# Attention and gated MLP on one core: v split in the layout of its product, gate in one step, 8 pairs instead of 12 transposed by TensorE

## The chip, the core and the metric

The kernel runs on one core of a Trainium2 chip. The core has TensorE (PE in the profile; PEld is its weight load), VectorE (DVE), ScalarE (ACT), GpSimd (POOL) and SyncE (SP), which here only issues DMAs. Every engine works through its own list of instructions in order. The metric is the device time of one execution in microseconds (us), the median of several runs.

## The reference, cut to what matters

```python
def _attn_ref(q, k, v, w1, b1, w2):            # B, H, S, D = 8, 8, 576, 64
    scores = 1/np.sqrt(D) * np.matmul(q, k.transpose(0, 1, 3, 2))
    rel = (pos[:, None] - pos[None, :])
    x = np.log1p(np.abs(rel)) / np.log1p(np.maximum(pos[:, None], 1.0))
    bias = np.maximum(x[..., None] @ w1 + b1, 0.0) @ w2       # [S, S, H]
    scores = scores + bias.transpose(2, 0, 1)[None]
    attn = exp(scores - max); attn = attn / (attn.sum(-1) + 1e-9)
    return np.matmul(attn, v)

def _moe_ref(x, w_val, conv_w, w_out):         # x: [8, 576, 512], 5 taps
    gate_pre = sum(conv_w[k] * xp[:, k:k + S, :] for k in range(5))
    gate = 1.0 / (1.0 + np.exp(-gate_pre))
    return gate * (x @ w_val) @ w_out
```

The attention output of the 8 heads, laid side by side, is the x of the second function.

## The kernel before

**Pairs.** The attention is done in 32 pairs of heads (8 batches, 4 pairs each). A pair n has four blocks c of 128 query rows; the 64 rows that are left of two successive pairs share a fifth block. For each block TensorE makes the logits (L698, L714 for the fifth), VectorE adds the bias and takes the row minimum (`logits`, L744), ScalarE takes the exponential with its row sum (`expo`, L756). So the logits (L744) come 18 to every two pairs, 288 in all, and they are used below as a clock: "the 54th logits" ends the sixth pair.

**T pairs and D pairs.** The exponentials must be turned before they are multiplied with v. `TRANS` says how, for two pairs at a time. In a T pair ("T" in `TRANS`; 12 of 32 before: pairs 0 to 7, 16, 17, 24, 25) they are normalised (`norm`, L801), turned by TensorE in float32, nine 128x128 squares a block (`tp`, L846), copied out of PSUM (`tev`, L206), and multiplied with v in float32 (`piece`, L915; `rem_mm`, L983). In a D pair (20 before) ScalarE casts them to float16 (`top`, L206), GpSimd or VectorE takes the rest that the cast lost (`rest`, `rest8`, L229), SP issues a DMA transpose of high and low part together, 18 squares (`swap`, L880, L883), TensorE multiplies float16 products (L915, L983), and the row sums are spread by small matmuls (`rb`, L960, L992) and multiplied in afterwards (`mu`, L970).

**v of a D pair** is loaded with head dimension on the partitions (L630), its maximum is taken for each partition (L633), it is scaled and split into two float16 parts (L646, L649), and both are turned by a DMA transpose of 10 squares (`vtr`, L660).

**MLP.** When the four pairs of a batch are done, the five taps of the convolution run (`taps`, L1104, and L1064, L1069), then the gate: a tanh (`sig`, L1116) and a step that makes a scaled sigmoid of it (`half`, L1121 on ScalarE, L1123 on the others, for each of 4 slices of 128 channels). TensorE multiplies x with w_val in three float16 products (L1170), VectorE multiplies by the gate (`gf`, L1180), the product is split (L206, L229) and multiplied with w_out (L1225).

**Order.** Nothing is scheduled at run time: `ORDER` is a compressed table that lists the tasks in the order in which they are recorded, and the engine of each one that can run on more than one. Buffers come from rings of the sizes in `BUFS`. The first part of the program makes the bias rows and stores them to DRAM (L328 to L393); they are read back from there (L415).

Of the kernel before, what the change touches and what calls it, by code (L numbers as in the profile page):

```python
# [12 lines left out]
F16 = mybir.dt.float16  # L13
# [30 lines left out]
TRANS = tuple(x == "T" for x in "TTTTDDDDTDDDTDDD")  # L44
BUFS = dict(w=13, d=6, pt=2, sp=2, ps=4, qk=2, rel=3, be=9, xp=2, xh=1, gh=1, gx=1)
ORDER = (
    'c-nPW0cav;n|60cGue!Bl8nhDnPex)BpJ<QGf5_!Nix}5u;35&a1RSE*ux$!_=7zxSg?l$d$@-M3+~~91s5#X!v+7t9`<m-9v1A6|6vac?qPo{Sg>Hhg8i{z!5;U1WA^WVaQEtb-'
    '}^q#^S<AV^L^ipI7tyMk5`o4^+r>J(G06_e5>7&y1jm_;cM2}p#Pmf#A3DCb5V!0)oaINiFBcuFC_;<Jk=kKGqy6+uxH~{-sup9aHlJcuVHj78BZ{-Trppf1$Tk-'
    '1*$CPNu_(4tUp*P*Z5GsG8~K)TfNe>G+K6tQ*iNuD209A_FJz<YIx8u;}q$!R>vJ8mk$*cn$Q$t@uVeD>h)6tX2a$jmieyTL5_Z@&{6+2S2!Ix=?R&-'
    '$jJS{aOB1binLOmL9L0^8zm(cx6n+k#Z~*!MuPPvQ{#NG(DnxXye3d83u0EPbsCk8P&guo6syf)X*RuBz140<!nSBE>2$g6j!fRgb+Vp#!kNl-al(&Py<{{%`r>J#Q09u1Sb65A1)gHWwKwd;jJKQa'  # L50
    'NOF+%Rb%Bq!kTS;=kE>rlEOtSsnJ+t(F8DSkPTVGG9JYgdYd2G@bm~zjs?O_*c{GlBAIcCb*q%k=O~h*8L4(wsyS?pmeMQ~?UqE$S#~eKdJki{cBeS*_Te77;>onfTk56YCi+U1<e<zrs~SI@%8cBZ'
    '^l<!fF4%Z0oX8hLShLkGL}O*a<>pI~Y-dm*NSg6{=Xu)m`uqW}uVNE}Oukx^{6E+&R3K=Tm9VqhD>yzKuv{qAAGn4;^KMVE5(>X7MzHEbd%f{qX;>cN<C-'
    'L2*2dntMwBX54erAPS$W=i7z>6hR*SVj6r<%zxZN%J1Mx&MA}gJgH5Q+vzDOj~>0l;PqnWIwSC?%zyOPc23n521mroT0mg`6Cj-mW%X%KyXBueG7#Tj=vd7;_zHQKfg+@x-'
    '($3$ESt2>#qJ1QI1m?vM$Wb2JoJRKeQy}pt&;Hp%c{lREB8rMdT+%3&;luXqlX$?MZf7R4<Fpn4W`H8?>HxtYT!x-KoNUA`EqIj(L14q<y^<ue7=ZmsJa*>LOqHB#0XeQBK8^S8-'
    'jM2|($9vuWmkqu%7zV>pmP_(N3MO}2lroZH-RNo@PFEykiP_|Qp+z;by*SIcJ>J}_ZHL~;_XTp$=_(0#Pjq?R6k2;8AHycosf-713@wN~&LPRwRKC#9=A4Sx&wrTCKB-'
# [55 lines left out]
PACE = (3.35, 1.88, 2, 1)  # L111
PARTS = ((0, 256), (256, 320))
TOP = 2.0**12
GDIV = 2.0**20
LEAST = float(np.array([0x38000000], np.uint32).view(np.float32)[0])


# [1207 lines left out]
```

## Time and profile before

| what | value |
|---|---|
| median of 3 runs | 693.33 us (692.54 to 694.25) |
| the profiled execution: its own time, its span | 698.68 us, 696.2 us |
| TensorE matmul busy | 659.1 us (95% of the span) |
| VectorE, ScalarE, GpSimd busy | 623.7 (90%), 593.1 (85%), 457.3 us (66%) |
| DMA queue of SP (q1) | 80.5% of 16 engines |
| mean granted TensorE clock | 0.995 |

The span is the time from the first to the last instruction of the profiled execution. Busy times are the union of an engine's instructions; two instructions that overlap on one engine count once, so the mean durations of groups add up to more than the busy time. The DMA share is the sum of the packets' times over 16 engines, so it can pass 1 where packets overlap.

### The profile page before, as it was taken

To read this page: it belongs to the slowest core of one execution; us is meant where nothing else is said; L and a number is where in the kernel's file an instruction comes from. 1 tells how busy PE (TensorE), PEld (TensorE's weight loads), DVE (VectorE), ACT (ScalarE), POOL (GpSimd) and SP (SyncE) were. 2 spreads that over 40 slices of the span, in tenths; PEclk is the share of its full clock that TensorE was granted. 3 is DMA by queue.
4 is the path that set the end of the run, shared out by engine and by line. 5 is a ranking of instruction groups with operands and counts; after the bars stand their busy time and mean duration, and the time that the engine had idled before them with its cause. 6 is when DMAs were issued, how large, how long until landed. Compare 5 with 4: busy or idle time off the path is not lost. (4 is left out here: it accounts for less than half of the span.)

```text
span 696.2 us, 17319 instructions
## 1 busy us (share of the span) xinstructions
PE 659.1 (95%) x6144; PEld 418.3 (60%) x6144; DVE 623.7 (90%) x1631; ACT 593.1 (85%) x1332; POOL 457.3 (66%) x637
## 2 busy tenths in 40 slices
PE   6998899999999999899999999988999999999897
PEld 1223576666665666566667766556676666566563
DVE  7999799999999989979988898989898999999862
ACT  6999688888999979978879988879978988999761
POOL 0113656568787778767877787767858888976431
PEclk9999999999999999999999999999999999999999
DMA  3999826322269999999896599999973999999812
GB/s 112 327 320 322 293 104 231 107 93 65 73 121 168 210 214 202 221 189 191 165 203 203 104 184 190 199 220 206 185 187 104 181 217 215 214 188 183 178 63 74
DMA packets 263302, 125.73 MB, mean 181 GB/s; under 512 B 239792, under 2 KB 240048, under 8 KB 263216
## 3 DMA queue, kind: packets, MB, share of 16 engines
q1 hardware_dynamic: 263072, 124.34, 80.5%
q8 instruction: 48, 0.79, 0.5%
q14 instruction: 38, 0.31, 0.2%
q10 hardware_dynamic: 144, 0.29, 0.2%
HBM read 44.64 MB, written 20.33 MB: 93 GB/s over the span
## 5 line engine op out<-in xcount | busy, mean ns | idle before, releaser
L756 ACT ACTIVATE t_d<-t_d,nm 128x576 f32<-128x576 f32 x288 | 222.0, 773 | 33.3 <-DVE nm L744 30.0
L229 POOL TENSOR_TENSOR t_d<-t_d 128x512 f16<-128x512 f32 (+1 forms) x211 | 202.6, 977 | 64.9 <-ACT t_d L206 41.8
L744 DVE CUSTOM_DVE_ANT_0 t_d<-t_sp,bias 128x576 f32<-128x576 f32 x256 | 185.8, 749 | 15.4 <-PE t_sp L698 10.3
L698 PE MATMUL t_sp<-t_qk 64*128 64x288 f32 x1024 | 172.4, 430 | 3.5 <-DMA t_qk<-qkd 1.7
L915 PE MATMUL t_ps<-t_pt,t_w 128*64 128x256 f16 (+1 forms) x1600 | 130.2, 309 | 8.8 <-DMA t_w<-t_w 4.3
L698 PEld LDWEIGHTS t_sp<-t_qk 64*128 64x128 f32 x1024 | 97.8, 186 | 52.2 <-DVE nm L744 15.8
L801 POOL TENSOR_SCALAR t_d<-t_d,rinv 128x576 f32<-128x576 f32 x94 | 75.0, 809 | 45.9 <-DVE rinv L784 35.2
L206 ACT CAST t_d<-t_d 128x576 f16<-128x576 f32 x145 | 94.2, 667 | 8.7 <-DMA t_pt<-t_d 3.0
L1170 PEld LDWEIGHTS <-wv 128*128 128x128 f16 x768 | 72.5, 98 | 32.8 <-issue 12.9
L1170 PE MATMUL t_ps<-xh,wv 128*128 128x320 f16 (+1 forms) x512 | 74.3, 286 | 2.3 <-DVE t_w L213 1.2
L915 PEld LDWEIGHTS <-t_w 128*64 128x64 f16 x1120 | 58.3, 111 | 21.0 <-issue 15.6
L846 PE MATMUL t_ps<-ident,t_d 128*128 128x128 f32 x486 | 67.0, 280 | 3.8 <-POOL t_d L801 2.3
L1104 DVE SCALAR_TENSOR_TENSOR t_ps<-t_xp,convw,t_ps 128x288 f32<-128x288 f32 x126 | 65.3, 518 | 2.7 <-ACT t_ps L1095 0.7
L846 PEld LDWEIGHTS t_ps<-ident,t_d 128*128 128x128 f32 x486 | 52.7, 141 | 24.5 <-POOL t_d L801 8.8
L1225 PE MATMUL t_ps<-wo,gh 128*128 128x512 f16 x256 | 61.5, 380 | 1.1 <-ACT gh L206 0.7
L206 ACT COPY t_pt<-t_ps 128x512 f32<-128x512 f32 (+1 forms) x121 | 53.4, 485 | 4.1 <-PE t_ps L846 3.5
L756 ACT ACTIVATION_READ_ACCUMULATOR t_d<-t_d,nm 128x1 f32 x288 | 55.2, 192 | 0.0
L347 PE MATMUL t_ps<-rel,w 128*32 128x288 f32 (+17 forms) x352 | 46.1, 495 | 4.0 <-DVE t_be L368 2.1
L915 PEld LDWEIGHTS t_ps<-t_pt,t_w 128*64 128x64 f32 x480 | 33.7, 137 | 24.1 <-issue 4.8
L328 DVE TENSOR_SCALAR rel<-gt,sct,nb 128x576 f32<-128x576 f32 (+17 forms) x106 | 47.0, 512 | 0.1
L229 DVE TENSOR_TENSOR t_d<-t_d 128x512 f16<-128x512 f32 (+1 forms) x59 | 41.9, 719 | 3.0 <-ACT t_d L206 2.6
L1225 PEld LDWEIGHTS <-gh 128*128 128x128 f16 x256 | 23.1, 98 | 32.6 <-issue 6.9
(140 smaller groups left out, 1076.8 us busy)
## 6 DMA issues: line engine op xcount, KB each, us to landing
t_qk<-qkd SPq DMA_DIRECT2D x32, 576.0 KB, 4.6
bias_d<-t_be SPq DMA_DIRECT2D x36, 295.5 KB, 4.7
bias<-bias_d SPq DMA_DIRECT2D x16, 576.0 KB, 6.2
out<-t_w SPq DMA_DIRECT2D x32, 256.0 KB, 3.6
t_w<-vd SPq DMA_DIRECT2D x20, 320.0 KB, 3.9
t_w<-vn SPq DMA_DIRECT2D x12, 320.0 KB, 4.7
t_d<-wvd SPq DMA_DIRECT2D x4, 512.0 KB, 3.7
t_d<-wod SPq DMA_DIRECT2D x4, 512.0 KB, 3.6
```

The costliest lines, as they stand in the source:

```text
L206: A.copy(out=out, in_=in_)
L229: (V if e == "V" else G).tensor_tensor(out=out, in0=in0, in1=in1, op=ALU.subtract)
L328: (G if e == "G" else V).tensor_scalar(out=rel[g].t[:, 0:w], in0=src, scalar1=sct[:, mm : mm + 1], scalar2=nb1, op0=ALU.mult, op1=ALU.max,)
L698: T.matmul(ts[a][:, j, 0:hw], lhsT=qk.t[r, c * P : (c + 1) * P], rhs=qk.t[r, x : x + hw], start=True, stop=True,)
L744: V.tensor_tensor_reduce(out=part(c, a).rearrange("p (j f) -> p j f", j=2), in0=sp.t[:, :, 0 : S // 2], in1=bias.rearrange("p (j f) -> p j ...
L756: A.activation(out=part(c, a), in_=part(c, a), func=AF.Exp, bias=nms[c][:, a : a + 1], scale=-1.0, accum_out=sums[c][:, a, 0:1],)
L801: (G if e == "G" else V).tensor_scalar(out=t, in0=t, scalar1=rinvs[c][:, a : a + 1], scalar2=1.0, op0=ALU.mult, op1=ALU.mult,)
L846: T.transpose(t[:, k * P : (k + 1) * P], es[c].t[:, (k0 + k) * P : (k0 + k + 1) * P], ident)
L915: T.matmul(po.t[r, 0:256], lhsT=vt.t[:, v, r], rhs=pt[:, x, :, :] if tr else pt[:, :, x, :], start=(t == 0 and m == 0), stop=(t == 4 and m ...
L1104: V.scalar_tensor_tensor(out=o, in0=x, scalar=wt, in1=t, op0=ALU.mult, op1=ALU.add)
L1170: T.matmul(pm.t[:, 0:w], lhsT=weights["wv"][wi][:, k, d * P : (d + 1) * P], rhs=xb.t[xi][:, k, 0:w], start=(q == 0 and k == 0), stop=(q == ...
L1225: T.matmul(pm.t, lhsT=gb.t[gi][:, k, o : o + P] if o < 256 else gx.t[gi][:, k, :], rhs=weights["wo"][wi][:, k, :], start=(q == 0 and k == ...
```

## The change

- `TRANS` has T for 4 entries instead of 6: pairs 6, 7, 16 and 17 become D pairs (24 D, 8 T).
- v of a D pair is loaded in the layout in which the product needs it (positions on the partitions). Its maximum is still taken for each partition, but one scale holds for the whole pair: TensorE transposes the column of maxima, spread over 128 columns (`vp_mm`, L642), and VectorE takes the maximum of each row (`vp_max`, L646). The two float16 parts are written straight into the tile of the product (`vhi`, `vlo`, L660, L663); `vtr` is gone.
- The gate is (tanh + 1) times the product in one VectorE instruction that reads PSUM (`gf`, L1186); `half` is gone. Its factor for each channel goes into w_val once, at the start: TensorE spreads it over the partitions (`w_cols`, L555), VectorE multiplies it in (`w_even`, L559).
- The scales of the weights and of a batch are turned with transposes in place of matmuls with the identity (L530, L579).
- `norm` of a T pair may run on ScalarE (18 of 72 do).
- Fewer small buffers (`sm` 8 for 16, `nm` and `rinv` 12 for 24, `rinvs` 8 for 10), one more in ring d; `TOP` and `GDIV` are smaller powers of two; `ORDER` is a new table for the new list of tasks.

```diff
-TRANS = tuple(x == "T" for x in "TTTTDDDDTDDDTDDD")
-BUFS = dict(w=13, d=6, pt=2, sp=2, ps=4, qk=2, rel=3, be=9, xp=2, xh=1, gh=1, gx=1)
+TRANS = tuple(x == "T" for x in "TTTDDDDDDDDDTDDD")
+BUFS = dict(w=13, d=7, pt=2, sp=2, ps=4, qk=2, rel=3, be=9, xp=2, xh=1, gh=1, gx=1)
...
-TOP = 2.0**12
-GDIV = 2.0**20
+TOP = 2.0**4
+GDIV = 2.0**12
...
+    def w_cols(e):
+        t = bank(cs)
+        for k in range(NK):
+            T.transpose(t[:, k * P : (k + 1) * P], gsc[:, k : k + 1].to_broadcast([P, P]), ident)
+
     def w_even(e, x, k):
         w = weights["wv"][x][:, k, :]
-        scalars(e, w, w, wrow[2][:, 0, k : k + 1], 1.0)
+        V.scalar_tensor_tensor(
+            out=w, in0=w, scalar=wrow[2][:, 0, k : k + 1], in1=cs.t, op0=ALU.mult, op1=ALU.mult
+        )
...
-            T.matmul(bank(tb)[:, 0:P], lhsT=bsc[:, b, 0:1].to_broadcast([P, P]), rhs=ident, start=True, stop=True)
+            T.transpose(bank(tb)[:, 0:P], bsc[:, b, 0:1].to_broadcast([P, P]), ident)
...
+            def vp_mm(e):
+                T.transpose(bank(tb)[:, 0:P], vcol[:, b, p : p + 1].to_broadcast([P, P]), ident)
+
+            def vp_max(e):
+                t = sc["t"] = smp.tile([P, 4], F32, name="vsc", tag="vsc", bufs=10)
+                V.tensor_reduce(out=t[:, 0:1], in_=tb.t[:, 0:P], op=ALU.max, axis=AX.X)
...
             def vhi(e):
-                A.activation(out=vhl.t[:, 0, :], in_=raw.t, func=AF.Copy, scale=sc["t"][:, 2:3])
+                new(vt, [P, 10, P], F16)
+                A.activation(out=vt.t[:, 0:5, :], in_=raw.t, func=AF.Copy, scale=sc["t"][:, 2:3])
...
-            def vtr(e):
-                new(vt, [P, 10, P], F16)
-                SP.dma_start_transpose(vt.t, vhl.t.rearrange("p a f -> p (a f)"))
-
...
-                A.activation(out=g, in_=g, func=AF.Identity, scale=c, bias=c)
...
-                    V.tensor_tensor(out=gf_.t[:, 0:w], in0=pm.t[:, 0:w], in1=gates[d].t[:, t0 : t0 + w], op=ALU.mult)
+                    V.scalar_tensor_tensor(
+                        out=gf_.t[:, 0:w],
+                        in0=gates[d].t[:, t0 : t0 + w],
+                        scalar=1.0,
+                        in1=pm.t[:, 0:w],
+                        op0=ALU.add,
+                        op1=ALU.mult,
+                    )
```

Three places show how the instructions move. The first is TensorE from the 60th logits on, in the kernel before (t_sp are logits, t_ps<-ident,t_d are squares of exponentials being turned, t_ps<-t_pt,t_w are products with v, t_ps<-t_d,t_w those of the fifth block):

```order
L698 MATMUL t_sp<-t_qk 128x288 x4
L846 MATMUL t_ps<-ident,t_d 128x128 x11
L915 MATMUL t_ps<-t_pt,t_w 64x256 x2
L714 MATMUL t_sp<-t_qk 64x288 x8
L983 MATMUL t_ps<-t_d,t_w 64x64 x10
L915 MATMUL t_ps<-t_pt,t_w 64x256 x18
L698 MATMUL t_sp<-t_qk 128x288 x4
L846 MATMUL t_ps<-ident,t_d 128x128 x8
L983 MATMUL t_ps<-t_d,t_w 64x64 x10
L698 MATMUL t_sp<-t_qk 128x288 x4
L846 MATMUL t_ps<-ident,t_d 128x128 x14
```

The same place in the changed kernel, where L859 is the L846 of before, L928 its L915, L996 its L983, and L642 the new transpose of the column of maxima:

```order
L708 MATMUL t_sp<-t_qk 128x288 x4
L928 MATMUL t_ps<-t_pt,t_w 64x256 x10
L724 MATMUL t_sp<-t_qk 64x288 x8
L859 MATMUL t_ps<-ident,t_d 128x128 x13
L642 MATMUL t_ps<-ident,vcol 128x128
L859 MATMUL t_ps<-ident,t_d 128x128 x5
L708 MATMUL t_sp<-t_qk 128x288 x4
L996 MATMUL t_ps<-t_d,t_w 64x64 x10
L928 MATMUL t_ps<-t_pt,t_w 64x256 x10
L708 MATMUL t_sp<-t_qk 128x288 x4
L996 MATMUL t_ps<-t_d,t_w 64x64 x10
```

The squares of pairs 6 and 7 are gone from here on, and what stands between two sets of logits is shorter.

The second place is SP where the first D pairs begin, before (t_w<-vd loads v, t_pt<-t_d and t_d<-t_d turn exponentials, t_w<-t_w turns v):

```order
L630 DMA t_w<-vd 128x640 x2
L880 DMA_TRANSPOSE t_pt<-t_d 128x18x128 x3
L660 DMA_TRANSPOSE t_w<-t_w 128x10x128
L880 DMA_TRANSPOSE t_pt<-t_d 128x18x128 x2
L608 DMA t_qk<-qkd 128x1152
L1243 DMA out<-t_w 128x512
```

And in the changed kernel:

```order
L636 DMA t_w<-vd 128x640
L893 DMA_TRANSPOSE t_pt<-t_d 128x18x128
L468 DMA t_d<-wod 128x1024
L893 DMA_TRANSPOSE t_pt<-t_d 128x18x128
L636 DMA t_w<-vd 128x640 x2
L615 DMA t_qk<-qkd 128x1152
```

The transposes of v no longer stand between those of the exponentials, and the first of these is issued while weights still load.

The third is VectorE in a D stretch before, from the maximum of one pair's v to the reciprocal of its scale (L633, L637, L643; L744 are logits, L1104 taps):

```order
L633 TENSOR_REDUCE vcol<-t_w 128x1
L1104 SCALAR_TENSOR_TENSOR t_ps<-t_xp,convw,t_ps 128x288 x2
L937 MEMSET t_xp 128x4x4
L1008 TENSOR_TENSOR t_xp<-t_xp,t_ps 128x64
L1104 SCALAR_TENSOR_TENSOR t_ps<-t_xp,convw,t_ps 128x288
L1104 SCALAR_TENSOR_TENSOR t_w<-t_xp,convw,t_ps 128x288
L637 TENSOR_SCALAR vsc<-vcol 128x1
L744 ISA t_d,nm<-t_sp,bias_1_90 128x576
L744 ISA nm 128x1
L643 RECIPROCAL vsc<-vsc 128x1
```

In the changed kernel the same chain has the new maximum over the turned column (L646) in it, before the scale and its reciprocal (L650, L656); between L639 and L646 TensorE must have run L642:

```order
L639 TENSOR_REDUCE vcol<-t_w 128x1
L754 ISA t_d,nm<-t_sp,bias_1_86 128x576
L754 ISA nm 128x1
L754 ISA t_d,nm<-t_sp,bias_1_86 128x576
L754 ISA nm 128x1
L216 SCALAR_TENSOR_TENSOR xl<-t_xp,bsc,xh 128x320 x2
L1021 TENSOR_TENSOR t_xp<-t_xp,t_ps 128x64
L228 TENSOR_TENSOR t_d<-t_d 128x512
L663 SCALAR_TENSOR_TENSOR t_w<-t_w,vsc 128x640
L646 TENSOR_REDUCE vsc<-t_ps 128x1
L650 TENSOR_SCALAR vsc<-vsc 128x1
L656 RECIPROCAL vsc<-vsc 128x1
```

The chain has one more link on VectorE, and two sets of logits and other work now stand between its first and its second maximum.

## Rows read from the trace of the kernel before

**Rows 1.** The page, parts 1 and 2: busy time; DMA share in 40 slices.
```profile
PE 659.1 (95%) x6144; PEld 418.3 (60%) x6144; DVE 623.7 (90%) x1631; ACT 593.1 (85%) x1332; POOL 457.3 (66%) x637
...
DMA  3999826322269999999896599999973999999812
```

**Rows 2.** Busy time by stretch: length; PE, PEld, DVE, ACT, POOL; clock, DMA share, GB/s.
```profile
0.00:154.50 154.50, 138.93 (x1098) 74.85 (x1099) 143.19 (x385) 131.43 (x310) 62.85 (x107) 0.99 0.65 215
154.50:499.30 344.80, 332.82 (x3258) 222.98 (x3257) 314.99 (x829) 306.70 (x685) 264.38 (x349) 1.00 0.90 175
499.30:696.20 196.90, 187.30 (x1793) 120.51 (x1791) 165.50 (x421) 155.01 (x338) 130.09 (x182) 1.00 0.79 164
```

**Rows 3.** Chain that ended last, a stretch of it: start, us, what.
```profile
585.13 1.17 PE t_sp L698 x8
586.30 5.00 PE t_ps L1170 x36
591.30 1.13 PE t_sp L714 x16
```

**Rows 4.** Groups by shape on TensorE: count, busy us, mean ns; idle before.
```profile
L915 PE MATMUL t_ps<-t_pt,t_w 128*64 128x256 f16 x1120 | 71.5, 276 | 6.4 <-DMA t_w<-t_w 4.3 <-DVE t_w L213 0.8 <-ACT t_w L1237 0.5
L846 PE MATMUL t_ps<-ident,t_d 128*128 128x128 f32 x486 | 67.0, 280 | 3.8 <-POOL t_d L801 2.3 <-ACT t_xp L206 0.8 <-ACT t_pt L206 0.2
L915 PE MATMUL t_ps<-t_pt,t_w 128*64 128x256 f32 x480 | 58.8, 387 | 2.4 <-DMA t_w<-vn 2.3
L960 PE MATMUL t_ps<-ident,rinvs 128*64 128x128 f32 x320 | 25.2, 280 | 2.4 <-ACT t_xp L224 2.1 <-DVE rinvs L784 0.3
L983 PE MATMUL t_ps<-t_d,t_w 128*64 128x64 f16 x560 | 12.8, 199 | 0.0
L983 PE MATMUL t_ps<-t_d,t_w 128*64 128x64 f32 x240 | 9.2, 225 | 0.0
L992 PE MATMUL t_ps<-ident,rinvs 128*64 128x64 f32 x80 | 6.5, 241 | 0.1
L572 PE MATMUL t_ps<-ident,bsc 128*128 128x128 f32 x16 | 3.5, 300 | 0.6 <-DVE t_w L1104 0.6
```

**Rows 5.** Groups by shape on VectorE.
```profile
L1104 DVE SCALAR_TENSOR_TENSOR t_w<-t_xp,convw,t_ps 128x288 f32<-128x288 f32 x42 | 21.6, 515 | 1.7
L1180 DVE TENSOR_TENSOR t_w<-t_ps,t_w 128x320 f32<-128x320 f32 x32 | 15.5, 484 | 5.8 <-PE t_ps L1170 5.6
L1180 DVE TENSOR_TENSOR t_w<-t_ps,t_w 128x256 f32<-128x256 f32 x32 | 13.2, 418 | 2.2 <-ACT t_w L1121 0.9 <-PE t_ps L1170 0.5 <-issue 0.5
L575 DVE TENSOR_REDUCE bsc<-t_ps 128x1 f32<-128x128 f32 x8 | 2.3, 282 | 0.0
```

**Rows 6.** Groups by shape on ScalarE.
```profile
L756 ACT ACTIVATE t_d<-t_d,nm 128x576 f32<-128x576 f32 x288 | 222.0, 773 | 33.3 <-DVE nm L744 30.0 <-POOL t_w L220 1.0 <-POOL t_w L219 0.7
L206 ACT CAST t_d<-t_d 128x576 f16<-128x576 f32 x145 | 94.2, 667 | 8.7 <-DMA t_pt<-t_d 3.0 <-POOL t_d L229 2.9
L206 ACT COPY t_pt<-t_ps 128x512 f32<-128x512 f32 x82 | 46.1, 588 | 2.6 <-PE t_ps L846 2.1 <-PE t_ps L915 0.2
L1121 ACT ACTIVATE t_w<-t_w,gsc 128x576 f32<-128x576 f32 x27 | 23.1, 858 | 0.2
```

**Rows 7.** Busy time by stretch: T pairs; then three stretches of D pairs.
```profile
75.00:194.00 119.00, 117.61 (x989) 80.50 (x986) 114.51 (x323) 104.24 (x263) 81.00 (x115) 1.00 0.38 129
194.00:370.00 176.00, 170.05 (x1695) 112.48 (x1695) 160.68 (x412) 154.32 (x340) 133.71 (x178) 0.99 1.00 191
400.00:515.00 115.00, 108.61 (x1105) 71.42 (x1102) 102.90 (x275) 97.94 (x216) 84.16 (x112) 1.00 1.09 201
540.00:650.00 110.00, 108.85 (x1082) 70.78 (x1079) 103.40 (x261) 99.88 (x219) 85.43 (x112) 1.00 1.03 199
```

**Rows 8.** DMA transposes on SP: issue time in ns (least/median/most); first, last start.
```profile
L880 SPq DMA_TRANSPOSE t_pt<-t_d x80: 2390/3128/5453, 194.3 to 652.6; - x80
L660 SPq DMA_TRANSPOSE t_w<-t_w x20: 1252/1391/2152, 206.1 to 650.6; - x20
```

More of the change, by code (lines that the diff above doesn't have):

```diff
@@ L298, in attention_gated_mlp @@
     consts = add([("V", 0.2)], constant_ev, [consts], -6, (), [pc])
-    sms, turn = [cp.tile([P, 10, 2], F32, name=f"sm_{i}") for i in range(16)], [0]
+    sms, turn = [cp.tile([P, 10, 2], F32, name=f"sm_{i}") for i in range(8)], [0]
     for t in sms:
@@ L530, in wg_mm @@
         for m in range(2):
-            T.matmul(
-                t[:, m * P : (m + 1) * P], lhsT=wsc[:, 4 + m : 5 + m].to_broadcast([P, P]), rhs=ident, start=True, stop=True
-            )
+            T.transpose(t[:, m * P : (m + 1) * P], wsc[:, 4 + m : 5 + m].to_broadcast([P, P]), ident)
     def wg_max(e):
@@ L547, in attention_gated_mlp @@
     wdone = add([("V", 0.12)], wg_row, wdone, last)
-    wdone = add([("P", 0.5)], wg_mm, [wdone], last, [wt_])
+    wdone = add([("P", 0.28)], wg_mm, [wdone], last, [wt_])
     wdone = add([("V", 0.4)], wg_max, [wdone], last, (), [wt_])
@@ L551, in attention_gated_mlp @@
     wdone = add([("G", 0.8)], wg_scales, [wdone], last)
+    cs = Buf("tt")
+    def w_cols(e):
+        t = bank(cs)
+        for k in range(NK):
+            T.transpose(t[:, k * P : (k + 1) * P], gsc[:, k : k + 1].to_broadcast([P, P]), ident)
     def w_even(e, x, k):
         w = weights["wv"][x][:, k, :]
-        scalars(e, w, w, wrow[2][:, 0, k : k + 1], 1.0)
-    wdone = [add([("V", 0.3), ("G", 0.7)], partial(w_even, x=x, k=k), [wdone], last) for k in range(NK) for x in range(2)]
+        V.scalar_tensor_tensor(
+            out=w, in0=w, scalar=wrow[2][:, 0, k : k + 1], in1=cs.t, op0=ALU.mult, op1=ALU.mult
+        )
+    wdone = add([("P", 0.5)], w_cols, [wdone], last, [cs])
+    wdone = [add([("V", 0.6)], partial(w_even, x=x, k=k), [wdone], last, (), [cs]) for k in range(NK) for x in range(2)]
     spilled, arrived, taker = {}, {}, {}
@@ L583, in batch_scale @@
         t = add([("V", 0.1)], vb_max, maxima[b], s0 + 1)
-        t = add([("P", 0.3)], vb_mm, [t], s0 + 1.5, [tb])
+        t = add([("P", 0.14)], vb_mm, [t], s0 + 1.5, [tb])
         t = add([("V", 0.25)], vb_all, [t], s0 + 2, (), [tb])
@@ L656, in vlo @@
                 )
[L658 to L660 removed]
             d = s0 - 1
[L663 removed]
+            t0 = add([("S", 0.9)], ldv, (), d - 1, [raw])
             t1 = add([("V", 0.74)], vmax, [t0], d)
             maxima.setdefault(b, []).append(t1)
[L666 removed]
+            t2 = add([("P", 0.14)], vp_mm, [t1], d + 0.2, [tb])
+            t2 = add([("V", 0.25)], vp_max, [t2], d + 0.3, (), [tb])
+            t2 = vscaled = add(SMALL, vscale, [t2], d + 0.5)
             t2 = add([("V", 0.08)], vinv, [t2], d + 0.6)
[L668 to L671 removed]
+            t3 = add([("A", 0.73)], vhi, [t2], d + 1, [vt])
+            tv = add([("V", 0.89)], vlo, [t3], d + 1.5, (), [raw])
         halves = [Buf("pt"), Buf("pt")]
@@ L1116, in sig @@
                 A.activation(out=gates[k].t, in_=gates[k].t, func=AF.Tanh, scale=0.5)
-        def half(e, k):
-            g, c = gates[k].t, gsc[:, k : k + 1]
-            if e == "A":
-                A.activation(out=g, in_=g, func=AF.Identity, scale=c, bias=c)
-            else:
-                (V if e == "V" else G).tensor_scalar(out=g, in0=g, scalar1=c, scalar2=c, op0=ALU.mult, op1=ALU.add)
         sg = []
@@ L1128, in mlp @@
             y = add([("A", 0.61)], partial(sig, ks=[k]), [convs[k]], x)
-            sg.append(add([("G", 0.77), ("A", 0.78), ("V", 0.5)], partial(half, k=k), [y] + wdone, x + 0.3))
+            sg.append(y)
         for pi, (t0, w) in enumerate(PARTS):
@@ L1206, in mlp @@
                     )
-                g1 = add([("V", 0.46)], gf, [v, sg[d]], x + 0.7, [gf_], [pm, gates[d]])
+                g1 = add([("V", 0.5)], gf, [v, sg[d]], x + 0.7, [gf_], [pm, gates[d]])
                 tk = []
@@ L1291 @@
     va = np.concatenate([va, va[..., NM * P :]], axis=3)
+    va = va.reshape(B, NP, P, 5, P).transpose(0, 1, 4, 3, 2).reshape(B, NP, P, RW)
     w1a = np.tile(np.asarray(inputs["w1"]).reshape(HID), 4).reshape(P, 1)
```

155 lines of the change are left out of this document (75 added, 80 removed).

## The prediction

> **What bounds the kernel now.** I read the page first. TensorE is busy 95% of the span, but VectorE 90% and ScalarE 85% [rows 1], so there is little slack behind it: the reader should see three engines within 66 us of each other, and a DMA row that changes between 2-3 and 9 with the kind of pair. Next the chain that ended last: where it runs on TensorE, one group begins in the microsecond in which the last one ends (585.13 + 1.17 = 586.30, then 5.00 to 591.30) [rows 3]. There TensorE issues without a gap, and work taken from it is time. The chain leaves it for VectorE, ScalarE and a transpose in other places, so this is not so everywhere.
>
> Then the busy times by stretch. I cut the span at the 54th and the 216th logits (154.5 and 499.3 us), since all four pairs that change kind lie between them. That stretch takes 344.8 us with TensorE busy 332.8, VectorE 315.0, ScalarE 306.7 [rows 2]: the busiest engine works 96.5% of it. In the T stretch TensorE reaches 98.8% beside a VectorE of 96.2%; in three D stretches TensorE has 96.6, 94.4 and 99.0% [rows 7].
>
> **The sum, TensorE.** A T pair costs it, in busy time by group [rows 4], 67.0/12 = 5.6 us of squares, 58.8/12 = 4.9 of float32 products and 9.2/12 = 0.8 for the fifth block: 11.3. A D pair costs 71.5/20 = 3.6 of float16 products, 12.8/20 = 0.6, and (25.2 + 6.5)/20 = 1.6 for the spread sums: 5.8. Four pairs: 4 x 5.5 = -21.8 us. Added are 24 turned maxima. The trace has no transpose of a spread column; a square of exponentials costs 67.0/486 = 0.14 us, the batch scale as a matmul 3.5/8 = 0.44 [rows 4]. The new instruction is the former in everything but its operand, so I take 0.14: +3.3 (bound +10.5). Spreading the gate's factor adds 4 x 0.14 = 0.6, the 8 batch scales save up to 8 x 0.3 = 2.4. TensorE: about -20 (-13 to -24), nearly all between 154.5 and 499.3: 332.8 becomes 312.
>
> **VectorE** does not get lighter there. Added: 24 maxima over the turned column at 0.28 [rows 5] = 6.8; four more low parts of v and four more pairs of `mu`, about 8.0; 64 gate products that become three-operand ones. A three-operand one with an operand in PSUM takes 0.515 at 288 columns, the plain product 0.418 at 256 and 0.484 at 320, so 0.45 at 288 [rows 5]: 64 x 0.065 = +4.1. The weights' factor is 8 three-operand ones of 512 columns in place of plain ones; by the row of 288 columns each lies between 0.515 and, in proportion, 0.92, so with the plain ones off I take +3.7 for all. Counting equal instructions in the two orders, the new table takes about 34 us of norms, rests, splits, copies and output scaling off VectorE, and gives it 9 of other kinds. Net -3 over the program, about 0 in the stretch: 315.
>
> **ScalarE** loses 27 gate steps, 27 x 0.86 = -23.2, and 28 large copies out of PSUM, -16.5 (with the small ones -26); it gains 43 casts x 0.667 = +28.7 [rows 6], 18 norms (the nearest row is the exponential of the same size, 0.773 [rows 6]) = +13.9, and +25 of splits, v's high parts and scaling. Net +18 by means, +15 after the overlap that the busy time leaves out; some +8 of it in the stretch: 315. The rest are mostly norms in the early T stretch, where ScalarE has 104 of 119 us [rows 7], so they cost nothing while that slack lasts; without it, 13 x 0.77 = 10 us. GpSimd stays at about 457: 44 more rests, 42 fewer norms. Fewer small buffers could add waits that I can't see; their users are 8 to 12 blocks apart, so I take none.
>
> **DMA.** SP issues 18 more transposes of 18 squares (108 for 90), 3.13 us each, and 20 fewer of 10, 1.39 each [rows 8]: +28 us of issue. For a single D pair it is less: 4.5 x 3.13 = 14.1 where it was 15.5. The v chain was load, maximum, scale, split, transpose; the transpose's landing goes, and TensorE's waits for it (4.3 us [rows 4]) with it; what is late next is `vlo`, which TensorE's products of that pair wait for. The new round trip over TensorE has two or more logits of other work on VectorE beside it in the order. Without that cover, each waiting L646 would hold the logits queued behind it on VectorE, and TensorE and ScalarE with them: about 0.5 us x 24 = 12.
>
> So the stretch ends with 312, 315 and 315 us on three engines. The busiest now sets it, and the question is how well it is fed. I take 95%: between the 94.4% of the worse D stretch and the 96.5% of today, near the lower because three engines at once must be busy. 315/0.95 = 331.6, that is -13; bounds 315/0.99 = 318 (-27) and 315/0.914 = 344.8 (0). Outside it the T pairs and the tail keep their work; TensorE has some 2 us more after the 234th logits, so I add +1. The profiled span of 696.2 would become 684. That execution itself took 698.68 where the runs have a median of 693.33; I carry the difference over: 693.3 - 12 = **681 us**.
>
> **Weighed against the Trainium skill.** For 128x128 the trace has 3.13 us of issue for 18 squares, 0.17 us a square, and TensorE 0.14 plus a copy [rows 4, 8]. The Trainium skill (VectorE: DVE Perf Modes, The three transpose paths) gives 390 ns for TensorE and 1309 ns for the DMA, and its rules for kernel authors say to use TensorE where PSUM will do. By that, 18 D pairs of 81 squares would need 1,900 us in this stretch, so its price doesn't hold here, though its direction speaks against the change; it is the last rival below. And the Trainium skill (Perfetto Trace Analysis, Identifying the Most-Contended Engine) calls the busy time of matmuls a poor measure of headroom and would take weight loads, here 60%; by it VectorE's 90% is the limit. The gapless chain [rows 3] contradicts it in places, and it is the second rival.
>
> **Rivals.**
> - *TensorE alone bounds.* For it: 99.0% in the last D stretch and 98.8% in the T stretch [rows 7]. Its -20 then counts in full at today's 96.5%: -21, 672 us. Against: the others rise to the same load.
> - *VectorE is already the limit*, with ScalarE after it: TensorE's waits are theirs. Its load doesn't change, so the stretch stays and the time is 693 (688 to 695). For it: 315 of 344.8. Against: the chain, and 96.2% of VectorE in the T stretch [rows 7].
> - *The transposes bound, and it gets slower.* 18 D pairs now follow each other, where T pairs, early and in the middle, had let the DMA engines rest [rows 1]. In 400 to 515 us they worked 1.09 x 115 = 125 us for 6 pairs, 20.9 a pair [rows 7]; without v's 10 of 91 squares, 18.8. For 18 pairs 338 engine-us. At a sustained share of 0.95 that is 356 us, +11, or 704; below 0.98 the change loses. Against: 1.09 and 1.03 were held for 115 and 110 us, and 1.00 for 176.
>
> **How the numbers follow.** What a measurement of this kernel can tell from no change is about 0.3%, or 2 us. Chances: the forecast (675 to 688) 0.48; TensorE alone (667 to 675) 0.17; still less 0.03; VectorE 0.17, of which 0.10 lies within 0.3% and 0.07 below; transposes 0.15. Faster 0.75, same 0.10, slower 0.15. The range, 669 to 695, leaves out part of the first rival and the last one.
>
> **What would show it.** In the changed profile: TensorE busy near 639, VectorE 621, ScalarE 608, GpSimd 457; the stretch from the 54th to the 216th logits near 332 us, with no engine above 97%; no wait of TensorE for t_w from a DMA transpose; the turned maxima at 0.14 us. Wrong would be: a stretch near 318 or 345, TensorE or VectorE waiting on DMA t_pt<-t_d for more than some us, L646 waiting for TensorE, or a start or tail that grows by more than 5 us.

## The result, and the profile after

The changed kernel takes 682.78 us (median of 4 runs, 681.59 to 684.14), the kernel before 693.79 on the same chip; the ratio is 0.984, 95% interval 0.982 to 0.987. The profiled execution took 684.14 us, its span is 682.3. That is 1.4 us above its median, where the profiled execution of the kernel before lay 4.9 above its own; so of the difference of the two spans, 13.9 us, some 3.5 may be spread between executions, and in which stretch they lie is not known. First the page of the changed kernel, as [rows 1], with the granted clock:

```profile
PE 643.9 (94%) x6176; PEld 409.8 (60%) x6176; DVE 620.4 (91%) x1630; ACT 603.7 (88%) x1353; POOL 454.0 (67%) x604
...
PEclk9999999999789999999999999999999999999999
DMA  7799844328788999999999999999975899998604
```

Against [rows 1] TensorE is 15.2 us lighter, VectorE 3.3, ScalarE 10.6 heavier. The DMA engines' rest in the middle is gone; the clock falls twice, near 175 and near 195 us (the 7 and the 8). Busy time by stretch, cut at the 54th and the 216th logits as in [rows 2], then the middle stretch cut at the 72nd and 90th:

```profile
0.00:147.80 147.80, 136.82 (x1075) 74.84 (x1075) 139.31 (x384) 134.62 (x307) 58.21 (x97) 1.00 0.68 224
147.80:487.70 339.90, 320.56 (x3294) 213.01 (x3294) 313.50 (x822) 315.15 (x704) 268.14 (x338) 0.98 1.00 196
487.70:682.30 194.60, 186.54 (x1814) 121.96 (x1810) 167.55 (x426) 153.91 (x344) 127.69 (x171) 1.00 0.74 154
...
147.80:188.50 40.70, 33.71 (x292) 21.53 (x290) 37.84 (x96) 35.23 (x82) 30.13 (x39) 0.92 0.70 151
188.50:226.90 38.40, 37.10 (x365) 25.36 (x364) 36.77 (x98) 36.83 (x82) 33.18 (x38) 0.96 0.91 178
226.90:487.70 260.80, 249.76 (x2641) 166.12 (x2640) 238.89 (x631) 243.09 (x542) 204.84 (x263) 1.00 1.06 206
```

The gain is not where it was forecast. By the medians it is 11.0 us. Of the 13.9 us of span, 6.7 come before the 54th logits, 4.9 in the middle, 2.3 behind it. The middle has two faces: its first 41 us, where TensorE works 33.71 of 40.70 us, and, from the 90th logits on, 261 us in which it works 95.8% and the DMA engines hold a share of 1.06. The groups that the sum had priced, answering to [rows 4 to 6]:

```profile
L859 PE MATMUL t_ps<-ident,t_d 128*128 128x128 f32 x324 | 44.9, 281 | 2.0 <-ACT t_pt L205 0.7 <-POOL t_d L814 0.6 <-ACT t_d L205 0.4
...
L1186 DVE SCALAR_TENSOR_TENSOR t_w<-t_w,t_ps 128x320 f32<-128x320 f32 x32 | 15.2, 479 | 6.1 <-PE t_ps L1176 6.1
...
L223 ACT ACTIVATE t_d<-t_d,rinv 128x576 f32<-128x576 f32 x18 | 14.1, 782 | 0.0
...
L1186 DVE SCALAR_TENSOR_TENSOR t_w<-t_w,t_ps 128x256 f32<-128x256 f32 x32 | 12.9, 410 | 1.4 <-PE t_ps L1176 1.4
...
L642 PE MATMUL t_ps<-ident,vcol 128*128 128x128 f32 x24 | 7.3, 305 | 2.1 <-ACT wo L498 2.1
```

A lone turned maximum (L642) costs 0.30 us, not 0.14; the norms on ScalarE (L223) cost the 0.78 that was taken. The gate's three-operand product costs what the plain one did (0.479 for 0.484, 0.410 for 0.418).

The stage that goes badly, at 165 to 185 us, in stretches of 5 us (columns as above), and the waits between the 54th and the 72nd logits (who, for what: us in total, times, longest):

```profile
165.00:170.00 5.00, 3.23 (x42) 1.93 (x38) 4.93 (x12) 4.84 (x12) 3.26 (x3) 1.00 0.91 211
170.00:175.00 5.00, 2.64 (x23) 1.76 (x23) 4.93 (x15) 3.06 (x8) 2.68 (x3) 0.72 1.03 208
175.00:180.00 5.00, 5.00 (x32) 3.13 (x30) 2.53 (x9) 1.95 (x4) 3.20 (x5) 0.60 0.75 143
180.00:185.00 5.00, 3.85 (x42) 2.38 (x38) 4.96 (x14) 5.00 (x13) 3.70 (x9) 1.00 0.52 98
```

```profile
PEld L928 <- DVE t_w L663: 2.2, 1, 2.2
PE t_ps L642 <- ACT wo L498: 2.1, 1, 2.1
...
PE t_ps L928 <- DVE wrow L489: 2.0, 1, 2.0
```

The second name in such a line is the one that came last by the profile. The instructions around the three waits (start, us) show which operand it was:

```profile
169.17 0.99 DVE L663 SCALAR_TENSOR_TENSOR t_w<-t_w,vsc 128x640 f16<-128x640 f32 x1
171.82 0.80 DVE L639 TENSOR_REDUCE vcol<-t_w 128x1 f32<-128x640 f32 x1
...
166.15 1.24 PE L708 MATMUL t_sp<-t_qk 64*128 64x288 f32 x8
170.22 0.41 PE L928 MATMUL t_ps<-t_pt,t_w 128*64 128x256 f16 x4 [1.99 <-DVE wrow L489]
172.77 0.45 PE L642 MATMUL t_ps<-ident,vcol 128*128 128x128 f32 x1 [2.14 <-ACT wo L498]
175.21 2.29 PE L708 MATMUL t_sp<-t_qk 64*128 64x288 f32 x8
```

VectorE is full (4.93 of 5 us). Between 162.2 and 169.2 us the steps of the weights' last block (L428 to L486) take 5.6 of its 7.0 us, two sets of logits most of the rest. In its queue behind them stand a pair's low part of v (L663, which ends at 170.16), which the products of that pair (L928, at 170.22) wait for, and the next pair's maximum (L639, which ends at 172.62), which L642 (at 172.77) waits for on TensorE, ahead of everything else there. TensorE works 3.23 and 2.64 of 5 us, then the granted clock is 0.60 for a stretch: most of it at the lower of the two levels, 1.2 GHz, and TensorE busy for all of it with 32 instructions. The same eight matmuls of logits (L708) take 2.29 us there and 1.24 before it. A second fall follows, to 0.66 between 192 and 197 us, in which TensorE is busy throughout.

### The profile page after: what moved, and what is told of

Its sections match the earlier page's. It is cut to its first block, busy times and chain, and to the rows that moved or that the text cites. A ratio compares the mean times of both kernels' runs of the same rounds, so it can differ in the third digit from the quotient of the medians.

```text
span 682.3 us, 17380 instructions
## 1 busy us (share of the span) xinstructions
PE 643.9 (94%) x6176; PEld 409.8 (60%) x6176; DVE 620.4 (91%) x1630; ACT 603.7 (88%) x1353; POOL 454.0 (67%) x604
## 5 line engine op out<-in xcount | busy, mean ns | idle before, releaser
L228 POOL TENSOR_TENSOR t_d<-t_d 128x512 f16<-128x512 f32 (+1 forms) x274 | 261.1, 974 | 68.7 <-ACT t_d L205 45.6
L708 PE MATMUL t_sp<-t_qk 64*128 64x288 f32 x1024 | 173.0, 432 | 5.5 <-DVE nm L754 3.4
L928 PE MATMUL t_ps<-t_pt,t_w 128*64 128x256 f16 (+1 forms) x1664 | 127.3, 300 | 8.2 <-DMA t_pt<-t_d 5.5
L708 PEld LDWEIGHTS t_sp<-t_qk 64*128 64x128 f32 x1024 | 97.9, 187 | 54.5 <-issue 15.2
L205 ACT CAST t_d<-t_d 128x576 f16<-128x576 f32 x188 | 121.4, 666 | 7.1 <-DMA t_pt<-t_d 3.5
L928 PEld LDWEIGHTS <-t_w 128*64 128x64 f16 x1344 | 70.5, 111 | 29.3 <-issue 19.8
L814 POOL TENSOR_SCALAR t_d<-t_d,rinv 128x576 f32<-128x576 f32 x52 | 41.0, 800 | 22.6 <-DVE rinv L794 13.5
L346 PE MATMUL t_ps<-rel,w 128*32 128x272 f32 (+17 forms) x352 | 48.2, 506 | 4.5 <-DVE t_be L367 2.6
L327 DVE TENSOR_SCALAR rel<-gt,sct,nb 128x560 f32<-128x560 f32 (+17 forms) x106 | 47.3, 517 | 0.1
L859 PE MATMUL t_ps<-ident,t_d 128*128 128x128 f32 x324 | 44.9, 281 | 2.0 <-ACT t_pt L205 0.7
L859 PEld LDWEIGHTS t_ps<-ident,t_d 128*128 128x128 f32 x324 | 34.9, 140 | 16.3 <-issue 6.9
L228 POOL TENSOR_TENSOR gl<-t_w,gh 128x256 f16<-128x256 f32 x47 | 34.0, 725 | 14.2 <-DVE gxl L228 6.9
L1176 PE MATMUL t_ps<-xl,wv 128*128 128x256 f16 (+1 forms) x256 | 40.7, 286 | 0.0
L223 ACT ACTIVATE t_xp<-t_ps,vsc 128x256 f32<-128x256 f32 (+1 forms) x72 | 28.8, 409 | 11.2 <-PE t_ps L1005 5.8
```

The source lines that it names most:

```text
L205: A.copy(out=out, in_=in_)
L228: (V if e == "V" else G).tensor_tensor(out=out, in0=in0, in1=in1, op=ALU.subtract)
L327: (G if e == "G" else V).tensor_scalar(out=rel[g].t[:, 0:w], in0=src, scalar1=sct[:, mm : mm + 1], scalar2=nb1, op0=ALU.mult, op1=ALU.max,)
L346: T.matmul(pb[32 * g : 32 * g + 32, 0 : y - x], lhsT=w28, rhs=rel[g].t[:, x:y], start=True, stop=True, tile_position=(0, 32 * g),)
L708: T.matmul(ts[a][:, j, 0:hw], lhsT=qk.t[r, c * P : (c + 1) * P], rhs=qk.t[r, x : x + hw], start=True, stop=True,)
L859: T.transpose(t[:, k * P : (k + 1) * P], es[c].t[:, (k0 + k) * P : (k0 + k + 1) * P], ident)
```

## Experiments

All were timed against the kernel before on the same chip. Line numbers in their rows are those of their own files. The "stages" below are the times between every 18th logits; where two kernels do the same things they agree within some 0.3 us (the first three of the changed kernel and of the seven made from it with the start untouched: 46.7 to 46.9, 37.2 to 37.3, 31.1 to 31.2), so a profile tells where an edit acted.

| kernel | median us | ratio to before, 95% interval | span |
|---|---|---|---|
| changed | 682.78 | 0.984 [0.982, 0.987] | 682.3 |
| gate_alone | 701.82 | 1.012 [1.009, 1.015] | 703.3 |
| gate_copied | 696.96 | 1.004 [1.001, 1.006] | 693.3 |
| v_alone | 706.35 | 1.018 [1.016, 1.021] | 707.5 |
| gate_and_v | 711.61 | 1.025 [1.023, 1.028] | 712.5 |
| norms_on_gpsimd | 689.31 | 0.992 [0.990, 0.995] | 687.3 |
| more_tensore | 690.60 | 0.994 [0.992, 0.997] | 686.7 |
| more_vectore | 692.03 | 0.998 [0.996, 1.000] | 692.7 |
| more_scalare | 687.01 | 0.990 [0.987, 0.993] | 684.5 |
| v_transposes_kept | 781.71 | 1.124 [1.119, 1.129] | 779.3 |
| v_transposes_late | 723.15 | 1.041 [1.038, 1.044] | 723.3 |
| vlo_earlier | 680.05 | 0.980 [0.977, 0.982] | 677.8 |
| no_turned_scale | 679.94 | 0.980 [0.977, 0.982] | 678.8 |

**The two new forms on the old table.** Each was put into the kernel before, its order kept but for what the new tasks need.

```diff
 gate_alone: half, L1121, out; gf as in the change; w_cols, w_even as in the change
 v_alone:    v of a D pair as in the change (vp_mm, vp_max in, vtr out)
 gate_and_v: both
```

> The kernel before, its pairs and its table, with the gate in one step alone. By the rows ScalarE loses 27 steps of 0.86 us (23 us), VectorE gains the weights' factor (3.7) and, since the changed profile shows the three-operand product at the price of the plain one, nothing for it; TensorE gains 0.6. If three engines share the load, TensorE, the busiest at 96.5% in the long stretch, hides most of ScalarE's relief: 689 to 693 us. If TensorE alone sets the time: 693 to 695. If VectorE does: 696 to 698. If ScalarE's work counted in full: near 671.

> The kernel before with the split of v in the layout of its product alone: 20 turned maxima at the 0.30 us of the changed profile (6.1 us of TensorE), 20 maxima over them (5.6 us of VectorE), and no transposes of v (20 of 1.39 us of issue less). If three engines share the load and the transposes of v were hidden: 693 to 699 us. If TensorE or VectorE alone sets the time: 698 to 700. If the transposes bind, their 28 us of queue come back in part: 683 to 690.

> The kernel before with both of these, so that the changed kernel differs from it by the kind of four pairs, the table and the small buffers alone. If what I say of the two holds, 690 to 696 us, and 8 to 13 us of the gain belong to the pairs and the table. If the gain came from the two new forms of work, 682 to 685, and the pairs and the table would be worth nothing.

All three missed, upwards: by the ratios 8, 13 and 18 us slower than before. For the gate one stage holds it: it took 40.3 us before (186.7 to 227.0) and 49.2 here (49.2 in gate_and_v too, 40.8 in v_alone); all other stages together are 1.8 us shorter, though ScalarE was busy 18.3 us less. Busy time in that stage of gate_alone, columns as above:

```profile
187.50:236.70 49.20, 44.03 (x360) 28.21 (x361) 40.03 (x96) 36.30 (x80) 27.83 (x42) 0.93 0.64 121
...
200.00:210.00 10.00, 7.00 (x45) 4.52 (x47) 6.71 (x16) 5.83 (x13) 4.76 (x7) 0.66 0.60 113
```

And of its waits there:

```profile
PE t_ps L844 <- DVE wv L550: 1.7, 1, 1.7
...
PE t_ps L844 <- ACT t_pt L194: 1.4, 1, 1.4
```

TensorE waits with a T pair's squares (L844) for a PSUM bank that the eight factors (L550) still read; in the 10 us shown the clock is 0.66. Giving that bank back early was the test:

```diff
+    def w_copy(e):
+        copy(e, new(cm, [P, 512], F32), cs.t)
...
-            out=w, in0=w, scalar=wrow[2][:, 0, k : k + 1], in1=cs.t, op0=ALU.mult, op1=ALU.mult
+            out=w, in0=w, scalar=wrow[2][:, 0, k : k + 1], in1=cm.t, op0=ALU.mult, op1=ALU.mult
```

> The kernel before with the gate in one step alone, as in the run of that, but with the spread factor copied by ScalarE from its PSUM bank into SBUF, and the bank given back at once. In that run the 8.9 us of loss lay in one stage, 187.5 to 236.7, where VectorE's eight factors kept the bank for 8 us beside a T pair's squares, and TensorE's clock fell to 0.66. If it is the bank: 690 to 695. If the factors' work on VectorE or the new form of the gate costs it: 699 to 703.

697.0 us: between the two. The stage falls from 49.2 to 44.1 and the clock stays at 1.00 in it, so the bank was some 5 us of the 8.9; 4 us are left that it doesn't explain.

v_alone has no such single stage. Its largest loss is in the stage from 387.9 to 430.9 us, 42.9 us for 37.3 before. TensorE waits 7.1 us in all ahead of the new transposes (L624), where L642 in the changed kernel waits once, 2.1 us:

```profile
PE t_ps L624 <- ACT t_w L1229: 3.4, 2, 1.7
PE t_ps L624 <- DVE vcol L621: 1.9, 1, 1.9
PE t_ps L624 <- DVE t_w L1172: 1.8, 2, 1.2
```

The forms are thus no gain on the old order, and gate_and_v to changed, 711.6 to 682.8, is what the four pairs, the new table and its norms on ScalarE bring together, with the scales turned by transposes and the new sizes of rings. Of these only the norms were tried alone (below); the pairs and the table were not taken apart: other kinds of pairs need a table of their own.

**Norms.** The 18 norms of ScalarE given to GpSimd, only the engine of 18 tasks in the table changed.

> The changed kernel with its 18 norms of ScalarE given to GpSimd, at the same places of the table: ScalarE 13.9 us lighter, GpSimd about as much heavier. The prediction let ScalarE's norms cost nothing while its slack in the T stretch lasts: then this is the same within 2 us (681 to 685). If ScalarE binds there: 670 to 678. If what waits is the square behind the norm, GpSimd's longer norm (about 1.0 for 0.77 us, and behind other work) makes it slower: 686 to 692.

The last case: 689.3 us (687.3 of span for 682.3). Of the 5.0 us 4.4 are lost by the 72nd logits, 3.1 of it in the T stretch, which ends at 150.9 in place of 147.8. Its waits from 116 to 193 us:

```profile
ACT t_pt L195 <- PE t_ps L849: 4.3, 5, 2.1
PEld t_ps L849 <- POOL t_d L804: 4.2, 5, 2.3
```

The squares (L849) wait for GpSimd's norms (L804), and ScalarE's copies for the squares. In the changed kernel the same two kinds of waits were 0.4 us (ScalarE) and 0.8 us (TensorE) over such a window. A norm takes GpSimd 0.82 us there and ScalarE 0.78 in the changed kernel, not the 1.0 that I had expected for GpSimd: what costs is the place behind other work in GpSimd's list, not the length of the norm.

**More work for one engine at a time**, some 0.5 us in each of 24 D pairs.

```diff
 more_tensore
-    T.transpose(bank(tb)[:, 0:P], vcol[:, b, p : p + 1].to_broadcast([P, P]), ident)
+    t = bank(tb)
+    for x in (0, 1, 2, 3, 0):
+        T.transpose(t[:, x * P : (x + 1) * P], vcol[:, b, p : p + 1].to_broadcast([P, P]), ident)
 more_vectore: vmax over raw.t[:, 0:3, :] ahead of that over all of raw.t
 more_scalare: vhi of raw.t[:, 0:3, :] ahead of that of all of raw.t
```

> The changed kernel with 0.56 us more for TensorE in each of the 24 D pairs: four transposes more of the same column, 13 us in all. If three engines share the load, with TensorE (320.6 of 339.9 us) the busiest by little, most of it counts: 8 to 14 us more, 691 to 697. If TensorE alone sets the time: 695 to 697. If VectorE does: 682 to 685.

> The changed kernel with about 0.5 us more for VectorE in each of the 24 D pairs: the maximum over three fifths of v taken once more, 12 us in all. If three engines share the load: TensorE has 7 us more to do in the stretch than VectorE, so 3 to 8 us more, 686 to 691. If TensorE alone sets the time: 683 to 684. If VectorE does: 694 to 696.

> The changed kernel with about 0.55 us more for ScalarE in each of the 24 D pairs: three fifths of v's high part written twice, 13 us in all. If three engines share the load: 3 to 8 us more, 686 to 691. If TensorE or VectorE alone sets the time: 683 to 684. If ScalarE does: 694 to 697.

By the groups, one of each of the three kernels, the added work is 10.4 us of TensorE (17.7 for 7.3), 12.9 of VectorE and 14.6 of ScalarE:

```profile
L634 PE MATMUL t_ps<-ident,vcol 128*128 128x128 f32 x120 | 17.7, 278 | 2.1 <-ACT wo L488 2.1
```

```profile
L630 DVE TENSOR_REDUCE vcol<-t_w 128x1 f32<-128x384 f32 x24 | 12.9, 539 | 0.0
```

```profile
L651 ACT ACTIVATE t_w<-t_w,vsc 128x384 f16<-128x384 f32 x24 | 14.6, 608 | 0.1
```

By the ratios, against the changed kernel's, they cost 6.9, 9.3 and 4.0 us, each +-2.4. So over the whole kernel 0.7 of an added microsecond counts on TensorE and on VectorE, 0.3 on ScalarE, each good to some 0.2. Against the cases: TensorE's 690.6 lies just under that of a shared load (691 to 697), VectorE's 692.0 between the shared load (686 to 691) and VectorE alone (694 to 696), ScalarE's 687.0 in the shared load. By place, 5.8 of VectorE's us are lost between the 54th and the 90th logits, the stretch with the weights' last steps on VectorE. TensorE's price holds falls of the clock: executions of more_tensore with a granted clock of 0.997 took 687.6 to 688.5 us, those with 0.987 to 0.993 took 690.2 to 691.6.

In the steady stretch, 260.8 us, the three cost 3.5, 2.7 and 2.2 us. 12, 12 and 13 of the 24 additions stand there (5.2, 6.5 and 7.9 us by the groups), and the engine's own busy time in it rises by 3.5, 7.3 and 7.5 us. vlo_earlier (below), with the changed kernel's work, takes 258.6 us for this stretch, so such a difference is good to some 2 us. That is against VectorE or ScalarE as the only limit there; it is not against TensorE, and it shows no order of the three.

**The transposes.** v's transposes kept, with a result that nothing reads.

```diff
+                new(raw, [P, 10, P], F16)
+                SP.dma_start_transpose(raw.t, vt.t.rearrange("p t d -> p (t d)"))
```

> The changed kernel with a transpose of 10 squares of v kept in each of the 24 D pairs, whose result nothing reads: 24 of about 1.39 us of issue and 24 x 10 squares for the DMA engines more, 11% of what they turn. If the transposes are hidden: 682 to 685 us. If they bind, the DMA engines' share of 1.0 in the long stretch says that it grows by up to a tenth: 700 to 715. If only their queue is at its limit here and there: 686 to 692.

> The changed kernel with the unused transpose of v once more, but issued some 40 tasks behind the low part that it waits for (in two pairs 4, in three 12 to 32), so that the queue of SP does not stand before it: in the run that kept the transposes it stood 77 us for them. If the 99 us came from the standing queue: 683 to 695. If the DMA engines are full, 240 squares more at the 0.16 us of issue that a square costs are 39 us: 705 to 725. If both, more than that.

Kept right behind `vlo` they cost 97 us by the ratios (99 by the medians), more than any case I had written: SP's queue stood 56.6 and 20.1 us before issues that were not ready, and the big transposes behind them. Issued late, in a task of its own, the same work costs 39 us, which is the case that I had written for full DMA engines. Busy time in the steady stretch of v_transposes_late:

```profile
229.40:524.10 294.70, 262.85 (x2632) 175.43 (x2631) 239.30 (x630) 245.31 (x543) 206.51 (x262) 0.94 1.04 200
```

Its unused transposes (issue in ns, least, median, most) and who waited for them longest:

```profile
L673 SPq DMA_TRANSPOSE t_w<-t_w x24: 1321/1366/2783, 173.2 to 680.7; - x24
...
...
  DVE t_w L1181: 12.4, 7
```

The stretch grows from 260.8 to 294.7 us for 13 transposes of 1.37 us of issue. With shares of 1.06 and 1.04 the DMA engines worked some 30 engine-us more in it (1.04 x 294.7 less 1.06 x 260.8), and it grew by 33.9. That fits DMA engines without room, but does not show it, for three other things hold too. SP's issues fill 230.4 of the 260.8 us in the changed kernel already (88%; 79% from 227.0 to 464.2 us of the kernel before), so SP's list may be what is full. The granted clock fell to 0.94, and TensorE was busy 13.1 us longer for the same work. And the unused result holds a buffer of ring w that later work waits for, 12.4 us on VectorE (the kept ones hold one too). What each of these costs was not separated. Engines' waits for the big transposes rise (ScalarE 4.0 to 18.0 us, TensorE 5.5 to 10.9, VectorE 0.5 to 7.6). The Trainium skill (VectorE: DVE Perf Modes, The three transpose paths) puts a 128x128 square at 1309 ns by DMA. The run's ten in one instruction took 1.37 us of issue and 3.9 us to landing (medians), so as a price for each square the figure doesn't hold here.

**The stalled stage.** Four tasks moved in the table:

```diff
 vhi of pair 7:  place 1001 -> 951     (ahead of the weights' last block)
 vlo of pair 7:  place 1026 -> 972
 vp_mm of pair 6: place 1049 -> 1068   (behind pair 7's first five products)
 vp_max of pair 6: place 1058 -> 1078
```

> The changed kernel with one place of its table changed, where the weights' last steps fill VectorE: the pair after the 54th logits gets its high and low part of v some 50 tasks earlier, and the next pair's turned maximum stands behind the products instead of ahead of them. The stage from the 54th to the 72nd logits took 40.6 us in the changed kernel, with TensorE waiting 2.0 and 2.1 us there and its clock down to 0.60 after it; the D stages behind it took 34.5 to 40.1. If it is these waits: 4 to 7 us less, 676 to 679. If VectorE is simply full there and another wait takes their place: 681 to 684.

680.05, between the two cases; ratio 0.980: it beats the kernel before, and by the medians the changed one, but the intervals of the two ratios touch (0.977 to 0.982, 0.982 to 0.987). The span is 4.5 us shorter. In the stage itself only 1.9 of them appear (40.6 to 38.7 us); the same 20 us as above:

```profile
165.00:170.00 5.00, 5.00 (x70) 3.63 (x68) 4.91 (x13) 4.28 (x12) 2.54 (x2) 1.00 0.74 185
170.00:175.00 5.00, 3.38 (x27) 1.68 (x23) 4.95 (x14) 3.88 (x10) 2.98 (x5) 1.00 0.90 169
175.00:180.00 5.00, 3.04 (x16) 2.01 (x18) 4.96 (x15) 4.92 (x11) 4.41 (x10) 0.83 0.91 173
180.00:185.00 5.00, 5.00 (x33) 2.93 (x31) 3.91 (x12) 4.02 (x9) 4.42 (x7) 0.50 0.53 86
```

TensorE's two waits are gone, but VectorE stays full for 15 us, TensorE then waits for the weights' scale (1.8 us), and the clock falls all the same, later, though once where it had fallen twice. Both cases had a part: the waits were worth 2 us where they stood, and VectorE is full there.

**The turned maxima**, left out; each partition then has its own scale, so the pair's common scale is not computed.

> The changed kernel without the turned maxima: each partition of v is scaled by its own maximum, so the common scale of a pair's rows is left out. TensorE loses 24 transposes (7.3 us by the rows), VectorE 24 maxima (6.7). By what 12 to 13 us of added work cost in the runs for it (0.6 of a TensorE microsecond, 0.75 of a VectorE one): 672 to 676. If their waits are all that counts (1.6 us for the maxima): 680 to 683.

679.94, just under the case of the waits: by the ratios 3.3 us less, +-2.4, not 9. Of its 3.5 us of span 2.0 lie in the stage that stalls (38.6 for 40.6). The price of the maxima is nearer to that of the waits (1.6 us) than to their 14 us of work on two engines; work taken away gave back less here than added work had cost.

## Why the prediction came out

**The total** was right, 681 for 682.8, and so was the forecast that TensorE's relief pays only in part. That the number came so near is luck in good part, for two errors cancelled: the middle stretch gave 4.9 us where I had 13, and the rest gave 9.0 where I had a loss of 1 (all of the span, with the 3.5 us of spread in them).

- *"315/0.95 = 331.6, that is -13"*: it took 339.9. Its engines came out at 320.6, 313.5 and 315.2 for 312, 315 and 315. At my feed of 95% TensorE's 320.6 alone would give 337.4, so 5.8 of the missing 8.3 us are TensorE's size and 2.5 the feed, which was 94.3%. Of TensorE's 8.6 us too many, 17 of the 24 turned maxima, at 0.30 us for 0.14, are some 2.7. I had taken 0.14 from squares that follow each other (67.0/486); the mean of one in the same row, 280 ns, was the nearer price for a lone one. The clock is an estimate of some 3 more: TensorE is busy 6.2 us longer at the lower level than before, where L708 took 2.29 us for 1.24. The other 3 are not found. The 94.3% is a mean of 82.8% in the stage that stalls, 96.6% in the next, and 95.8% in the steady stretch, and I had no term for the first: the last weights stand ahead of `vlo` on VectorE. I had named `vlo` as what is late next, and not looked for what stands before it.
- *"For a single D pair it is less: 4.5 x 3.13 = 14.1 where it was 15.5."* Right in sign, and I took nothing for it. With such transposes issued late the changed kernel takes 723 us, some 28 slower than before; so the gain would not stand with them, though why (DMA engines, SP's list, clock, buffer) is argued and not shown. The rival *"The transposes bound, and it gets slower"* had the load right, 338 engine-us for a measured 340 (1.00 x 339.9), and missed on the share that can be sustained: not 0.95, but 1.00 over the stretch and 1.06 over 261 us of it. One of my signs of being wrong is there: TensorE waits 5.5 us, in five waits, for the big transposes (0.4 before).
- *"So they cost nothing while that slack lasts"* (norms on ScalarE): they are a gain; given back to GpSimd, they cost 5.6 us by the ratios. I had looked at ScalarE's slack alone, and not at what waits for the norm. With that, *"Outside it the T pairs and the tail keep their work"* failed: 3.1 of the 6.7 us before the 54th logits are these norms. The rest was not taken apart. Behind the 216th logits the first stage goes from 32.1 to 29.5 us, and to 30.3 in gate_alone, so there the gate's new form may have part in it.
- *"64 x 0.065 = +4.1"* for the gate products on VectorE: -0.6. But VectorE's busy time is 620.4 for 621, so some other term of that sum was as much too low; which is not known. ScalarE has 603.7 for 608, GpSimd 454 for 457, TensorE 643.9 for 639.
- *"The new round trip over TensorE has two or more logits of other work on VectorE beside it in the order."* VectorE waited 1.6 us for L642 in all, so on that side it is hidden; on the other, TensorE waited once, 2.1 us, for the maximum.
- *TensorE alone, or VectorE alone, as the limit*: over the whole kernel neither, since a microsecond more costs 0.7 on either (+-0.2), 0.3 on ScalarE. In the steady stretch TensorE alone isn't excluded. The Trainium skill (Perfetto Trace Analysis, Identifying the Most-Contended Engine) distrusts a busy matmul row as a measure of headroom; here that busy share, 94%, went with a price of 0.7, as did VectorE's 91%.

**Open:** how much the kinds of the four pairs bring apart from the table; whether v's transposes cost by the DMA engines or by SP's list; what gate_copied still loses in its stage; and why vlo_earlier gains 2.6 us behind its stage.

## What to carry to other kernels

Price a new form of work with the order refitted to it: on the old order these two forms cost 2.5%, on the new one they are part of a 1.6% gain. Before a long stretch is forecast by its busiest engine, look in it for the one place where an in-order queue is full of something that happens once (here the weights), and for the resource that is not an engine's row (here, as far as the runs go, the DMA transposes: a share of 1.06, and SP issuing for 88% of the time). And when work is given to another engine, ask who waits for its result, not only whether the engine has time.

## What the hardware showed

- A transpose of a spread column costs TensorE 0.30 us alone, but four more behind it only 10.4/96 = 0.11 us each.
- A three-operand VectorE instruction with one operand in PSUM and a constant scalar takes the time of the plain two-operand one (0.479 and 0.410 us at 320 and 256 columns).
- TensorE was busy 3.23 of 5 us at a granted clock of 1.00 (165 to 170 us), 2.64 of 5 at 0.72, then all of 5 at 0.60, and 3.85 of 5 at 1.00 again: the low clock outlasted the waits. Eight matmuls that took 1.24 us at the higher level took 2.29 there.
- The DMA engines' share, as the profile counts it, held 1.06 for 261 us; the prediction had asked whether 0.98 could be held. That 1.06 is their limit is not shown.
